# Two results of an MLP block scaled in two units, and the recurrent part's first preparations put one block earlier

## The chip, the cores and the metric

The kernel runs on one core of a Trainium2 chip. The core has TensorE (matrix products, PE in the profile; its weight loads are PEld), VectorE (DVE), ScalarE (ACT), GpSimd (POOL) and SyncE (SP), each with its own queue of instructions, and 16 DMA engines. The metric is the time of one execution in microseconds (us), as the median of several runs.

## The reference

Two mixers over the same 2048 rows of 512 numbers, joined by a gate. Cut to what matters:

```
g = sigmoid((x * gate_w).sum(-1))
a = A(x)          # recurrent attention: 64 segments of 32 rows, 32 heads of 128
b = B(x)          # layernorm, 512 -> 1376, gelu, 1376 -> 512
return g * a + (1 - g) * b

A: mem = mem0                                  # 8 memory rows
   for each segment xs:
       h = concat(mem, xs)                     # 40 rows
       q, k, v = h @ Wq, h @ Wk, h @ Wv
       o = softmax(mask(q @ k.T * scale)) @ v @ Wo
       mem, out = o[:8], o[8:]
```

The segments depend on one another through the memory rows, so A is a chain of 64 steps. B and the gate have no such chain.

## The kernel before, in words

The order of all instructions is written out by hand: an engine takes them in the order in which the program issues them, and waits only where data or a buffer isn't ready. There are two parts. First comes the MLP (B) together with the gates, some 98 us long, during which the weights of A are loaded; then the loop of 64 steps, about 10.4 us each.

**The MLP.** It goes in 8 blocks (`blk`, 0 to 7) of two tiles of 128 rows. A block has 11 units (`fc`, 0 to 10), one for each 128 of the 1376 hidden numbers. A unit does two things (loop over `units`):
- `a_mm(blk, fc)`: four products into PSUM bank SbF or W, by turns (line 460), then ScalarE's GELU from that bank into hTm (line 461). The bank is free again when the GELU has read it, so the products of unit n + 2 wait for the GELU of unit n.
- `b_mm` of the unit two before (LAG = 2): two products (line 466), one for each tile, added up over the 11 units in two of the four banks U. Even blocks use U[0] and U[1], odd ones U[2] and U[3].

A block's last `b_mm` thus stands in unit 1 of the next block. There the two results are scaled by 1 - g and written to SBUF as `ct` (ScalarE, line 473), and stored to the scratch tensor `c_dr` by a DMA that GpSimd issues (line 476). In the last block VectorE scales (line 475) and SyncE issues the store.

Other work is put between the units. In unit 0: ScalarE's tanh for the gates of the block before (line 449) with two small VectorE steps, then `prep` for the next block: statistics of its two tiles, a reciprocal square root in small steps, and the normalized tiles y (line 432), all on VectorE. In units 6 and 7: `prep_tr` (7 and 8 in block 0), the transposes of y on TensorE into banks X1 and X2 (line 439), which VectorE copies to yT (line 440). In unit 8: `loads`, which issues transfers of later tiles and of A's weights on SyncE's queue. In block 3 these include the first two transposed tiles xT (line 94) and the memory rows m0 (line 346).

**What leads over to the loop.** Of each segment's 32 rows, 24 ride with the 8 memory rows in one 32-column tile hT; the last 8 ("left rows") of four segments are gathered into a tile GL and multiplied together. The generator `first()` does the preparations for the first four segments in the last block, as side work between the units:
- its first piece, in unit 1: four small transposes of m0 into X1 (line 481); VectorE's copy of them into hT (line 482) is put into a list that is emptied right after; `left_x` for two tiles (the copies of left rows into GL by GpSimd, line 99); `prep_h(0)`, the copy of 24 rows into the first hT by GpSimd (line 237);
- then 24 pieces of four products each (`left_v`, line 139, and `left_qk`, line 120), six groups of four pieces, in banks X1, X2, U[0], X1, X2, U[0]. The table `(0, 1, 1, 0, 0, 8, 0, 8, 0, 8, 0)` says how many pieces each unit takes: one in unit 1, one in unit 2, eight in units 5, 7 and 9.

**The loop.** Each step projects hT to q, k and v, does the scores, the exponentials, the weighted sums and the product with Wo, and writes the new memory into the next hT. The left rows of later tiles are side work in it.

The code of the functions that the change touches, with the line numbers that the profile uses:

Of the kernel before, what the change touches and what calls it, by code (L numbers as in the profile page):

```python
# [10 lines left out]
BF16 = mybir.dt.bfloat16  # L11
I32 = mybir.dt.int32
ACTF = mybir.ActivationFunctionType
ALU = mybir.AluOpType
# [13 lines left out]
def kernel(ctx, tc, A_x, A_mem0, A_Wq, A_Wk, A_Wv, A_Wo, A_seg_len, B_x, B_w1, B_b1, B_w2, B_b2, gate_w, out):  # L28
    nc = tc.nc
    P = 128  # L30
    _, S, Dm = A_x.shape
# [15 lines left out]
    RIDE = 32 - M  # L47
# [3 lines left out]
    scale = float(Dh) ** -0.5  # L51
# [12 lines left out]
    c_dr = dram.tile([S, Dm], BF16, name="c_dr")  # L64
# [6 lines left out]
    hT = [ep.tile([P, KC, 32], BF16, name=f"hT{i}") for i in range(3)]  # L71
# [19 lines left out]

    def load_xT(T):
        xT = ew.tile([P, KC, P], BF16, tag="xT", bufs=3, name="xT")
        nc.sync.dma_start_transpose(out=xT[:], in_=x2[T * P:(T + 1) * P, :])
        xTs[T] = xT

    def left_x(T):
        GL = ew.tile([P, KC, LEFT, SPT], BF16, tag="GL", name="GL")
        nc.gpsimd.tensor_copy(out=GL[:].rearrange("p k c i -> p k i c"), in_=xTs[T][:].rearrange("p k (i t) -> p k i t", i=SPT)[:, :, :, RIDE:seg])
        GLs[T] = GL  # L100

# [55 lines left out]
    dve_q, act_q = [], []  # L157

    def flush(q, n=1):
        for _ in range(min(n, len(q))):  # L160
            q.pop(0)()
# [4 lines left out]
    def left_qk(T, t, hf, bk):  # L166
        for kc in range(KC):
            qk_unit(bk, gl(T), t, hf, kc)
            if kc < KC - 1:
                yield  # L170
        def ca():
            Tb = qk_cast(bk[:])
            dve_q.append(lambda: qk_tr(Tb, QL[T % 2], hf) if t == 0 else kl_tr(Tb, T, hf))
        act_q.append(ca)
        yield
# [6 lines left out]
    def left_v(T, vb, bk):  # L182
        if vb == 0:
            VLs[T] = ew.tile([P, 4, 2, Dh], BF16, tag="VL", bufs=1, name="VL")
        for kc in range(KC):
            v_unit(bk, gl(T), vb, kc)
            if kc < KC - 1:
                yield

        def ca():  # L190
            VL = VLs[T]
            nc.scalar.copy(out=VL[:, :, vb, :], in_=bk[:].rearrange("p (a e) -> p a e", a=4))

            if vb == 1:
                vp_load(T, 0)
        act_q.append(ca)
        yield
# [37 lines left out]
    def prep_h(s):  # L235
        T, si = divmod(s, SPT)
        nc.gpsimd.tensor_copy(out=hT[s % 3][:, :, 0:RIDE], in_=xTs[T][:, :, seg * si:seg * si + RIDE])
# [54 lines left out]
    with tc.tile_pool(name="mlpw", bufs=1) as mlpw, \  # L292
         tc.tile_pool(name="mwork", bufs=2) as mwork, \
         tc.tile_pool(name="msmall", bufs=2) as msmall:
        TB = 2
        NBLK = NT // TB
# [9 lines left out]
        def ld_x(T, eng=nc.sync):  # L306
            xt = mwork.tile([P, Dm], BF16, tag="xt", bufs=6, name="xt")
            eng.dma_start(xt[:], x2[T * P:(T + 1) * P, :])
            xts[T] = xt

        def ld_w(W_, A, n):
            nc.sync.dma_start(W_[:, n, :], A[n * P:(n + 1) * P].rearrange("p h e -> p (h e)"))

        def ld_o(i):
            nc.sync.dma_start(Wo_sb[:, i:i + 8, :], A_Wo[i:i + 8].rearrange("h e d -> e h d"))
# [23 lines left out]
        def loads(blk):  # L339
            if 2 * blk + 7 < NT:  # L340
                ld_x(2 * blk + 6)
                ld_x(2 * blk + 7)
            if blk == 3:
                for T in range(2):
                    load_xT(T)
                nc.sync.dma_start(m0[:], A_mem0[0])

            for kc in range(2 * blk, min(2 * blk + 2, 3 * KC)):
                ld_w(*((Wv_sb, A_Wv), (Wq_sb, A_Wq), (Wk_sb, A_Wk))[kc // KC], kc % KC)
            if blk == 6:  # L350
                for i in range(0, H, 8):
                    ld_o(i)
# [46 lines left out]
        omg = mlpw.tile([P, NT], FP32)  # L399
# [42 lines left out]
        def gate_sums(blk):  # L442
            for T in range(blk * TB, blk * TB + TB):
                junk = mwork.tile([P, Dm], BF16, tag="junk", bufs=1, name="junk")
                nc.vector.scalar_tensor_tensor(out=junk[:], in0=xts.pop(T)[:], scalar=1.0, in1=gw_bc[:], op0=ALU.mult, op1=ALU.mult, accum_out=z_all[:, T:T + 1])

        def gates(blk):
            t0, t1 = blk * TB, blk * TB + TB
            nc.scalar.activation(out=th[:, t0:t1], in_=z_all[:, t0:t1], func=ACTF.Tanh, scale=0.5)
            nc.vector.tensor_scalar(out=g_all[:, t0:t1], in0=th[:, t0:t1], scalar1=0.5, scalar2=0.5, op0=ALU.mult, op1=ALU.add)  # L450
            nc.vector.tensor_scalar(out=omg[:, t0:t1], in0=th[:, t0:t1], scalar1=-0.5, scalar2=0.5, op0=ALU.mult, op1=ALU.add)

        def bp(blk, tt):
            return U[2 * (blk % 2) + tt]

        def a_mm(blk, fc):
            rows = min(P, F - fc * P)
            hp = (SbF, W)[(blk * FC + fc) % 2]
            for kc in range(KC):
                nc.tensor.matmul(hp[:rows, 0:TB * P], lhsT=w1_sb[:, kc, fc * P:fc * P + rows], rhs=yTs[blk][:, kc, :], start=(kc == 0), stop=(kc == KC - 1))  # L460
            nc.scalar.activation(out=hTm[blk % 2][:rows, fc, :], in_=hp[:rows, 0:TB * P], func=ACTF.Gelu_apprx_tanh, bias=b1_sb[:rows, fc:fc + 1], scale=1.0)

        def b_mm(blk, fc):
            rows = min(P, F - fc * P + 1)
            for tt in range(TB):
                nc.tensor.matmul(bp(blk, tt)[:], lhsT=hTm[blk % 2][:rows, fc, tt * P:(tt + 1) * P],  # L466
                                 rhs=w2_sb[:rows, fc, :], start=(fc == 0), stop=(fc == FC - 1))
            if fc == FC - 1:
                for tt in range(TB):
                    T = blk * TB + tt  # L470
                    ct = mwork.tile([P, Dm], BF16, tag="ct", bufs=4, name="ct")
                    if blk < NBLK - 1:
                        nc.scalar.activation(out=ct[:], in_=bp(blk, tt)[:], func=ACTF.Copy, scale=omg[:, T:T + 1])
                    else:
                        nc.vector.tensor_scalar(out=ct[:], in0=bp(blk, tt)[:], scalar1=omg[:, T:T + 1], scalar2=None, op0=ALU.mult)
                    (nc.gpsimd if blk < NBLK - 1 else nc.sync).dma_start(c_dr[T * P:(T + 1) * P, :], ct[:])

        def first():
            m0p = X1[:].bitcast(BF16)[:, 0:KC * M].rearrange("p (k m) -> p k m", k=KC)
            for kc in range(KC):  # L480
                nc.tensor.transpose(m0p[:, kc, :], m0[:, kc * P:(kc + 1) * P], ident[:M, :M])
            dve_q.append(lambda: nc.vector.tensor_copy(out=hT[0][:, :, RIDE:32], in_=m0p))
            for T in range(2):
                left_x(T)
            prep_h(0)
            yield
            bks = (X1, X2, U[0], X1, X2, U[0])
            for n, (v, t, hf) in enumerate(((1, 0, 0), (1, 0, 1), (0, 0, 0), (0, 1, 0), (0, 0, 1), (0, 1, 1))):
                yield from (left_v(0, hf, bks[n]) if v else left_qk(0, t, hf, bks[n]))
# [15 lines left out]
        for n, (blk, fc) in enumerate(units):  # L505
            a_mm(blk, fc)
            if n == len(units) - 1:
                dummy = msmall.tile([P, 1], FP32, tag="dummy", name="dummy")
                nc.scalar.activation(out=dummy[:], in_=omg[:, 0:1], func=ACTF.Exp)
            if n >= LAG:  # L510
                b_mm(*units[n - LAG])
            if fc == 0:
                if blk >= 1:
                    gates(blk - 1)
                if blk + 1 < NBLK:
                    prep(blk + 1)
                else:
                    gate_sums(blk)
            if blk + 1 < NBLK:
                f0 = 7 if blk == 0 else 6  # L520
                if fc in (f0, f0 + 1):
                    prep_tr(blk + 1, fc - f0)
                if fc == f0 + 1:
                    gate_sums(blk)
                if fc == 8:
                    loads(blk)
                if fc == 9:
                    next(cgen, None)
            elif fc >= 1:
                if fc == 1:  # L530
                    side0 = first()
                if fc == 3:
                    gates(blk)
                for _ in range((0, 1, 1, 0, 0, 8, 0, 8, 0, 8, 0)[fc]):
                    next(side0, None)
                    flush(act_q, 9)
                    flush(dve_q, 9)
# [108 lines left out]
    for s in range(nseg):  # L646
        T, si = divmod(s, SPT)
# [254 lines left out]
```

## Time and profile before

| | |
|---|---|
| median of 3 runs | 780.51 us (779.76 to 783.5) |
| the profiled execution | 779.49 us |
| its span, first to last instruction | 777.7 us |
| TensorE busy | 761.1 us (98%) |
| ScalarE busy | 529.5 us (68%) |
| VectorE busy | 345.1 us (44%) |
| GpSimd busy | 278.7 us (36%) |
| mean granted TensorE clock | 0.997 of full speed |

Times in the views count from the first instruction. A row of the timeline has the start, the length, the engine, the line, the instruction with its output and inputs, and in brackets the idle time of the engine before it and what ended that. "x2" in such a row merges two instructions into one stretch. Matmuls are pipelined, so the length of a merged row is longer than the time until the next row starts. In the view of groups, a row ends with the busy time in all and the mean of one in ns. In the view of stretches, a row has the length, then the busy time of each engine (PE, PEld, DVE, ACT, POOL), the clock, the DMA share and GB/s. In the table of waits the three numbers are the time in all, the times and the longest.

### The profile page before, as it was taken

The numbers are of one execution on the slowest core, as the hardware profiler recorded it, in microseconds if no ns is written. First come the engines' busy times: TensorE is split into PE (matmuls) and PEld (weight loads), VectorE is DVE, ScalarE is ACT, GpSimd is POOL, SyncE is SP. The second block draws the span as 40 slices with busy tenths as digits, with TensorE's granted clock in tenths as the row PEclk, the third lists the DMA queues.
The fourth block names the chain that finished last, engine by engine and source line by source line (L and its number), as shares of the span: only waits on it lengthen the run. The fifth ranks groups of instructions, "written<-read, shape, count | busy, mean of one in ns | idle before, by whom it ended". The sixth has DMA issues, their size and how long they took to land.

```text
span 777.7 us, 44316 instructions
## 1 busy us (share of the span) xinstructions
PE 761.1 (98%) x19687; PEld 420.3 (54%) x19687; DVE 345.1 (44%) x1235; ACT 529.5 (68%) x1439; POOL 278.7 (36%) x523
## 2 busy tenths in 40 slices
PE   7999999999999999999999999999999999999996
PEld 5666555555555555555555555555555555555553
DVE  5776254344435343434443443534343444444334
ACT  4666576777777677777777677767777777777663
POOL 4111033433443433344433334434324443343342
PEclk9999999999999999999999999999999999999999
DMA  6779412212122222212221212222231212121221
GB/s 195 271 245 390 139 58 62 75 61 79 62 62 71 79 72 68 80 52 72 62 88 61 89 62 56 67 79 72 71 80 58 70 54 88 62 82 62 66 62 48
DMA packets 53174, 70.61 MB, mean 91 GB/s; under 512 B 21289, under 2 KB 42898, under 8 KB 51442
## 3 DMA queue, kind: packets, MB, share of 16 engines
q1 hardware_dynamic: 51250, 64.84, 26.0%
q8 instruction: 156, 2.56, 1.3%
q0 software_dynamic: 784, 1.97, 0.7%
q10 hardware_dynamic: 944, 0.92, 0.3%
q14 instruction: 40, 0.33, 0.1%
HBM read 56.96 MB, written 4.45 MB: 79 GB/s over the span
## 4 chain that ended last, share of the span: by engine, by line
PE 87%; DVE 1%; ACT 0%; issue 0%; DVEq 0%
PE U L120 29%; PE X L139 18%; PE W L151 15%; PE X L120 8%; PE X L151 4%; PE U L281 3%; PE U L640 2%; PE U L268 1%; PE W L257 1%; PE SbF L257 1%; PE W L249 1%; PE SbF L600 1%; PE SbF L249 1%; PE U L286 1%; PE U L466 1%; PE U L221 0%
## 5 line engine op out<-in xcount | busy, mean ns | idle before, releaser
L626 POOL TENSOR_TENSOR UT<-XR,Rb 128x384 bf16<-128x384 bf16 x126 | 140.1, 1133 | 296.2 <-DMA Rb<-r_dr 215.9
L125 ACT CAST Tb<-U 128x512 bf16<-128x512 f32 x258 | 150.8, 585 | 76.3 <-PE U L120 75.3
L120 PEld LDWEIGHTS <-hT 128*32 128x32 bf16 x4096 | 104.6, 96 | 109.3 <-DVE hT L642 16.3
L139 PE MATMUL X<-Wv_sb,hT 128*32 128x512 bf16 x2048 | 151.2, 379 | 0.0
L120 PE MATMUL U<-Wq_sb,hT 128*32 128x512 bf16 x2048 | 133.3, 380 | 0.5 <-DVE hT L642 0.2
L120 PE MATMUL U<-Wk_sb,hT 128*32 128x512 bf16 x2048 | 132.7, 379 | 0.0
L151 PE MATMUL W<-Wo_sb,UT 128*32 128x512 bf16 x2080 | 125.2, 380 | 1.3 <-ACT UT L718 1.2
L642 DVE CAST hT<-U 128x16 bf16<-128x16 f32 x126 | 21.9, 175 | 206.0 <-PE U L640 198.3
L129 DVE STREAM_TRANSPOSE QT<-Tb 128x256 f32<-128x256 f32 x128 | 57.0, 446 | 80.8 <-ACT Tb L125 80.7
L151 PEld LDWEIGHTS <-UT 128*32 128x32 bf16 x2080 | 59.4, 96 | 55.6 <-issue 16.3
L606 ACT CAST XR<-U 128x256 bf16<-128x256 f32 x252 | 78.6, 438 | 0.0
L129 DVE STREAM_TRANSPOSE KT<-Tb 128x256 f32<-128x256 f32 x128 | 57.0, 446 | 46.2 <-ACT Tb L125 46.0
L633 ACT CAST w<-W 128x256 bf16<-128x256 f32 (+1 forms) x128 | 41.9, 378 | 47.3 <-PE W L151 47.3
L626 POOL TENSOR_TENSOR UL<-XR,Rb 128x128 bf16<-128x128 bf16 x126 | 60.4, 503 | 0.0
L618 POOL TENSOR_TENSOR racc<-racc,R 128x72 f32<-128x72 f32 x63 | 21.2, 337 | 107.1 <-PE U L286 75.0
L139 PEld LDWEIGHTS <-hT 128*32 128x32 bf16 x2048 | 48.2, 94 | 21.0
L718 ACT CAST UT<-U 128x64 bf16<-128x64 f32 x252 | 35.3, 227 | 28.3 <-PE U L286 28.3
L710 ACT CAST V<-X 128x512 bf16<-128x512 f32 x64 | 37.4, 585 | 22.5 <-PE X L139 22.5
L466 PE MATMUL U<-w_sb,hTm 128*128 128x512 bf16 (+1 forms) x176 | 52.7, 383 | 0.0
L460 PEld LDWEIGHTS <-w_sb 128*128 128x128 bf16 (+1 forms) x352 | 34.2, 101 | 20.5 <-issue 3.2
L696 ACT CAST V<-X 128x512 bf16<-128x512 f32 x64 | 37.5, 585 | 9.5 <-PE X L139 1.1
L125 ACT CAST Tb<-X 128x512 bf16<-128x512 f32 x62 | 36.9, 595 | 7.8 <-PE X L120 6.0
(159 smaller groups left out, 1168.4 us busy)
## 6 DMA issues: line engine op xcount, KB each, us to landing
Rb<-r_dr SPq DMA_DIRECT2D x63, 512.0 KB, 3.9
Wv_sb<-in_A_Wv_dram SPq DMA_DIRECT2D x4, 1024.0 KB, 7.5
Wq_sb<-in_A_Wq_dram SPq DMA_DIRECT2D x4, 1024.0 KB, 7.2
Wk_sb<-in_A_Wk_dram SPq DMA_DIRECT2D x4, 1024.0 KB, 9.2
Wo_sb<-in_A_Wo_dram SPq DMA_DIRECT2D x4, 1024.0 KB, 15.1
VP<-VL SPq DMA_DIRECT2D x64, 64.0 KB, 3.2
c<-c_dr SPq DMA_DIRECT2D x16, 128.0 KB, 3.2
out_dram<-o SPq DMA_DIRECT2D x16, 128.0 KB, 2.7
```

The source lines that it names most:

```text
L120: nc.tensor.matmul(bk[32 * j:32 * j + 32, :], lhsT=G[:, kc, :], rhs=W5[t][:, kc, h0:h1, j, :], start=(kc == 0), stop=(kc == KC - 1), tile_ ...
L125: nc.scalar.copy(out=Tb[:], in_=bk.rearrange("p (a b e) -> p a e b", a=8, b=2))
L129: nc.vector.transpose(out=dst[:, 8 * hf:8 * hf + 8, c0:c0 + 32, :].rearrange("p a r b -> p a (r b)").bitcast(FP32), in_=Tb[:].rearrange("p ...
L139: nc.tensor.matmul(bk[32 * j:32 * j + 32, :], lhsT=G[:, kc, :], rhs=Wv5[:, kc, 4 * vb:4 * vb + 4, j, :], start=(kc == 0), stop=(kc == KC - ...
L151: nc.tensor.matmul(bk[32 * c:32 * c + 32, :], lhsT=U_[:, j, i, :], rhs=Wo_sb[:, 4 * i + j, :], start=(n == 0), stop=(n == NW - 1), tile_po ...
L466: nc.tensor.matmul(bp(blk, tt)[:], lhsT=hTm[blk % 2][:rows, fc, tt * P:(tt + 1) * P], rhs=w2_sb[:rows, fc, :], start=(fc == 0), stop=(fc = ...
L606: nc.scalar.copy(out=XR[:, j], in_=U[j][:, 0:NG * 40].rearrange("p (i q) -> p i q", q=40)[:, :, 0:32])
L626: nc.gpsimd.tensor_tensor(out=out[:, :, 4 * h:4 * h + 4, o:o + b - a], in0=XR[:, :, 4 * h:4 * h + 4, a:b], in1=Rb[:, h, :, :, a:b], op=ALU ...
L633: nc.scalar.copy(out=w[:, a:a + Dm // parts], in_=W[:, a:a + Dm // parts])
L696: nc.scalar.copy(out=v_out(V, 0), in_=X1[:])
L710: nc.scalar.copy(out=v_out(V, 1), in_=X2[:])
L718: nc.scalar.copy(out=UT[s % 2][:, j, :, 0:M], in_=U[j][:, 0:NG * 40].rearrange("p (i q) -> p i q", q=40)[:, :, 32:40])
```

## The change

Two things are put elsewhere; no instruction is added or taken away.

First, of a finished block's two results (blocks 0 to 6) the first is scaled and stored where both were, in unit 1 of the next block. The second goes into the list `late`, which is emptied one unit later, in unit 2, behind that unit's `a_mm` with its GELU and ahead of its `b_mm`. The last block still does both at its end.

Second, what was the first piece of `first()` becomes `first_h()`, and is called in unit 4 of block 6, behind that unit's products, instead of unit 1 of block 7. VectorE's copy into hT is issued there directly. The table for block 7 now has no pieces in units 1 and 2, so the 24 pieces of four products lie eight each in units 5, 7 and 9.

```
             if fc == FC - 1:
-                for tt in range(TB):
-                    T = blk * TB + tt
-                    ct = mwork.tile([P, Dm], BF16, tag="ct", bufs=4, name="ct")
-                    if blk < NBLK - 1:
-                        nc.scalar.activation(out=ct[:], in_=bp(blk, tt)[:], func=ACTF.Copy, scale=omg[:, T:T + 1])
-                    else:
-                        nc.vector.tensor_scalar(out=ct[:], in0=bp(blk, tt)[:], scalar1=omg[:, T:T + 1], scalar2=None, op0=ALU.mult)
-                    (nc.gpsimd if blk < NBLK - 1 else nc.sync).dma_start(c_dr[T * P:(T + 1) * P, :], ct[:])
-
-        def first():
+                if blk < NBLK - 1:
+                    ct_out(blk, 0)
+                    late.append(lambda: ct_out(blk, 1))
+                else:
+                    for tt in range(TB):
+                        ct_out(blk, tt)
+
+        late = []
+
+        def ct_out(blk, tt):
+            T = blk * TB + tt
+            ct = mwork.tile([P, Dm], BF16, tag="ct", bufs=4, name="ct")
+            if blk < NBLK - 1:
+                nc.scalar.activation(out=ct[:], in_=bp(blk, tt)[:], func=ACTF.Copy, scale=omg[:, T:T + 1])
+            else:
+                nc.vector.tensor_scalar(out=ct[:], in0=bp(blk, tt)[:], scalar1=omg[:, T:T + 1], scalar2=None, op0=ALU.mult)
+            (nc.gpsimd if blk < NBLK - 1 else nc.sync).dma_start(c_dr[T * P:(T + 1) * P, :], ct[:])
+
+        def first_h():
             m0p = X1[:].bitcast(BF16)[:, 0:KC * M].rearrange("p (k m) -> p k m", k=KC)
             for kc in range(KC):
                 nc.tensor.transpose(m0p[:, kc, :], m0[:, kc * P:(kc + 1) * P], ident[:M, :M])
-            dve_q.append(lambda: nc.vector.tensor_copy(out=hT[0][:, :, RIDE:32], in_=m0p))
+            nc.vector.tensor_copy(out=hT[0][:, :, RIDE:32], in_=m0p)
             for T in range(2):
                 left_x(T)
             prep_h(0)
-            yield
+
+        def first():
             bks = (X1, X2, U[0], X1, X2, U[0])
...
             a_mm(blk, fc)
...
+            while late:
+                late.pop(0)()
             if n >= LAG:
                 b_mm(*units[n - LAG])
...
                     loads(blk)
+                if blk == NBLK - 2 and fc == 4:
+                    first_h()
...
-                for _ in range((0, 1, 1, 0, 0, 8, 0, 8, 0, 8, 0)[fc]):
+                for _ in range((0, 0, 0, 0, 0, 8, 0, 8, 0, 8, 0)[fc]):
                     next(side0, None)
```

## The prediction

> **What bounds the kernel now.** I write (b,f) for unit f of MLP block b. First the page: TensorE works almost without a break, 98% of a span of 777.7 us, at a granted clock that no slice shows below 9 tenths. So time is gained only where TensorE stands still.
>
> ```profile
> span 777.7 us, 44316 instructions
> PE 761.1 (98%) x19687; PEld 420.3 (54%) x19687; DVE 345.1 (44%) x1235; ACT 529.5 (68%) x1439; POOL 278.7 (36%) x523
> PEclk9999999999999999999999999999999999999999
> ```
>
> Second, TensorE's waits in the first 160 us (time in all, times, longest). One row lies near the change: 1.5 us, once, for GL, the first left rows that GpSimd copies at line 99. No wait for an eviction of the scaled results (ct, line 473) is listed.
>
> ```profile
> PE X L139 <- POOL GL L99: 1.5, 1, 1.5
> ```
>
> Third, the timeline of that place, (7,1) and (7,2): start, length, engine, line, instruction.
>
> ```profile
> 80.79 0.60 PE L466 MATMUL U<-w_sb,hTm 97*128 97x512 bf16 x2
> 81.32 0.25 PE L481 MATMUL X<-ident,m 8*128 8x8 bf16 x4
> 81.50 0.61 PE L460 MATMUL W<-yT,w_sb 128*128 128x256 bf16 x4
> 81.95 0.59 PE L466 MATMUL U<-w_sb,hTm 128*128 128x512 bf16 x2
> 82.40 1.12 POOL L476 DMA_DIRECT2D c_dr<-ct  x2 [9.02 <-ACT ct L473]
> 83.56 0.74 POOL L99 COPY GL<-xT 128x128 bf16<-128x128 bf16 x2
> 84.08 0.40 PE L139 MATMUL X<-Wv_sb,GL 128*32 128x512 bf16 x4 [1.53 <-POOL GL L99]
> 84.11 0.27 POOL L237 COPY hT<-xT 128x96 bf16<-128x96 bf16 x1
> 84.41 0.61 PE L460 MATMUL SbF<-yT,w_sb 128*128 128x256 bf16 x4
> ```
>
> GpSimd issues two stores of ct (1.12 us), which wait for ScalarE's two evictions, and only then copies GL. TensorE meets its first left product at (7,2) and stands until the first copy is done. Its inputs are not late: the loads of xT started at 48.9 and 50.2 us and took at most 4.1, that of the memory rows started at 51.5.
>
> ```profile
> L94 SPq DMA_TRANSPOSE xT<-in_A_x_dram x2: 1242/1282/1322, 48.9 to 50.2; - x2
> DMA to landing us min/median/max: 2.8/3.5/4.1
> L346 SPq DMA_DIRECT2D m<-in_A_mem_dram x1: 480/480/480, 51.5 to 51.5; - x1
> ```
>
> Fourth, an ordinary block, here block 6. Blocks repeat to 0.02 us, so one stands for blocks 2 to 6.
>
> ```profile
> 28.80:38.95 10.15, 10.15 (x75) 6.96 (x74) 7.29 (x31) 6.19 (x15) 1.08 (x2) 1.00 0.74 259
> 69.36:79.49 10.13, 10.13 (x76) 6.95 (x74) 6.70 (x26) 6.23 (x15) 1.08 (x2) 1.00 1.05 376
> ```
>
> ```profile
> 70.65 0.17 DVE L450 TENSOR_SCALAR g_all<-th 128x2 f32<-128x2 f32 x1 [1.93 <-ACT th L449]
> ...
> 71.29 1.26 ACT L473 ACTIVATE ct<-U,omg 128x512 bf16<-128x512 f32 x2
> 71.96 0.60 PE L460 MATMUL W<-yT,w_sb 128*128 128x256 bf16 x4
> 72.27 1.12 POOL L476 DMA_DIRECT2D c_dr<-ct  x2 [9.02 <-ACT ct L473]
> 72.40 0.59 PE L466 MATMUL U<-w_sb,hTm 128*128 128x512 bf16 x2
> 72.43 0.48 ACT L461 ACTIVATE hTm<-SbF,b_sb 128x256 bf16<-128x256 f32 x1
> 72.79 0.49 ACT L461 ACTIVATE hTm<-W,b_sb 128x256 bf16<-128x256 f32 x1
> 72.97 0.60 PE L460 MATMUL SbF<-yT,w_sb 128*128 128x256 bf16 x4
> 73.40 0.59 PE L466 MATMUL U<-w_sb,hTm 128*128 128x512 bf16 x2
> 73.83 0.60 PE L460 MATMUL W<-yT,w_sb 128*128 128x256 bf16 x4
> 74.98 0.74 DVE L432 TENSOR_SCALAR y<-xt,mv,rs 128x512 bf16<-128x512 bf16 x2
> 75.14 0.59 PE L466 MATMUL U<-w_sb,hTm 128*128 128x512 bf16 x2
> 75.45 0.33 PEld L439 LDWEIGHTS <-y 128*128 128x128 bf16 x4 [0.21 <-DVE y L432]
> 75.57 0.39 PE L439 MATMUL X<-ident,y 128*128 128x128 bf16 x4
> ```
>
> A unit is two halves of 0.43 us, 0.87 in all (72.97 to 73.40 to 73.83). From 71.96 to 72.97 are 1.01 us: the products of (6,4) want bank SbF, whose GELU stood behind both ct and ended at 72.91 (72.43 + 0.48). That stall is 0.14 us. But look on: the transposes of y for the next block start at 75.57, right behind (6,6) (75.14 + 0.43), and their weight load had waited for y until 75.45. VectorE reaches y by a chain of small steps that begins right after ScalarE's tanh at the block's start (70.65) and runs for 4.3 us until the first y; a TensorE that is earlier at (6,6) waits for y.
>
> **The change part by part.** Nothing is added but order.
>
> *One ct moved behind the GELU of the next unit, blocks 1 to 5.* ScalarE's pitch is 0.57 for ct (71.29 to 72.43 for two), 0.36 for a GELU (72.43 to 72.79). The GELU of (b,2) then starts at 71.86 instead of 72.43, the second ct at 72.22, the GELU of (b,3) at 72.79 as now: it ends at 73.28, and its bank is wanted at 73.70. So the 0.14 stall goes. What is late next is y: the load can't start before 75.45, and its 0.1 us, which today lies under the matmuls, shows; the first useful effect is at about 75.55 against 75.57. Value 0.02 a block, five blocks: -0.1. Bounds: 0 and -0.7 (five times the whole 0.14). The store of the second ct comes some 0.4 us later on GpSimd's queue, where nothing but the moved copies stands behind it.
>
> *Memory transposed in block 6.* At (7,1) the four transposes cost 81.50 - 80.79 - 0.43 = 0.28 us; that goes: -0.28. At (6,4) the same 0.28 comes. There the products start at 72.83, the transposes follow at 73.80, and TensorE is ready for y's transposes at 75.72. These write X1, which VectorE must first have emptied of the memory rows. That copy (line 482, 170 ns) is queued behind both y: it starts about 0.33 us (the pitch of the two in 0.74, one taking 411) behind the second one's start, at 75.64, ends at 75.81, and the release reaches TensorE some 0.06 later (as from the first y's end, 74.98 + 0.41, to the load at 75.45), 75.87. So the transposes start at 75.87 instead of 75.57: +0.30. Bounds: +0.14 (0.28 less the stall, no wait for X1) and +0.77 (a y delayed by one GL copy, below).
>
> ```profile
> L432 DVE TENSOR_SCALAR y<-xt,mv,rs 128x512 bf16<-128x512 bf16 x4 | 1.5, 411 | 0.1
> L99 POOL COPY GL<-xT 128x128 bf16<-128x128 bf16 x2 | 0.7, 470 | 0.0
> L482 DVE COPY hT<-X 128x32 bf16<-128x32 bf16 x1 | 0.2, 170 | 0.0
> ```
>
> *GL and first hT copied in block 6.* GpSimd is idle there but for the stores of ct: today they start 0.3 us behind the first ct's end (72.27, against 71.29 + 1.26 - 0.57); counted the same way from the second ct's new end (72.22 + 0.69), the second store runs from 73.2 to 73.75. The three copies, 0.82 us now (83.56 to 84.38), then run to about 74.6. First use is at (7,5), over ten units later: nothing on the path. The cover that hides them is that distance; without it they would cost what (7,2) shows. SP's queue is not touched.
>
> *First left step taken out of (7,2).* From the end of the second half (81.95 + 0.43 = 82.38) to the next products at 84.41 are 2.03 us: the wait of 1.53, the work, and the changes of array shape on both sides. The work doesn't vanish; the sides take 8 steps each at units 5, 7 and 9, and unit 9 gets one step more than its seven. 28 products from 87.12 to 88.64 make 54 ns each, a step of four 0.22. Net -1.81; bounds -1.53 (the wait alone) and -1.81.
>
> ```profile
> 87.12 1.70 PE L139 MATMUL X<-Wv_sb,GL 128*32 128x512 bf16 x28
> 88.64 0.39 PE L120 MATMUL U<-Wq_sb,GL 128*32 128x512 bf16 x4
> ```
>
> What the standstill covered lies bare at (7,4): the late GELU would now stall it by 0.14, and the moved ct prevents just that, so nothing is added.
>
> Sum: -0.1 + 0.30 - 0.28 - 1.81 = -1.9 us, bounds -1.0 and -2.6. The profiled execution took 779.49 us and would take 777.6. The median of the runs, 780.51, is 1.0 above it, and the prediction is for the median: 778.6.
>
> **The rivals.** *The split pays in full:* y is not what TensorE waits for, because its chain moves too. Against it is the 0.21 us wait for y at 75.45. Then 0.14 - 0.02 more in five blocks, 0.6: 778.0.
>
> *A GL copy in y's way:* if GpSimd starts its copies late, a 470 ns copy could lie on y's start at 74.98, and y's transposes come 0.47 later: 779.1. By the sum GpSimd is done 0.4 us earlier; no row shows both at once. The Trainium skill (SBUF — State Buffer, Who interferes with whom) says that GpSimd shares a port pair with VectorE in its two-port modes, and that whoever issues second is blocked for the whole instruction; the trace of before cannot show this, since here the two never met.
>
> *The standstill moves on:* something that the wait at (7,2) hid stops TensorE for the same 1.53 later in block 7: sum -0.4, 780.1. Against it: apart from GL, none of TensorE's waits between 76 and 98 us is listed.
>
> *Slower:* the loop of 64 steps is entered 1.9 us earlier, with its transfers in another phase. In some steps the last matmul runs straight into the next step; in others hT comes last, for 0.19 us. These rows of the chain (start, us, what) show one of each:
>
> ```profile
> 108.42 0.45 PE X L120 x8
> 108.87 3.45 PE U L120 x64
> ...
> 129.13 0.19 DVE hT L642
> ```
>
> Ten more such steps eat the gain, 31 more make it slower by 0.5%; with half the steps, 32, it is 6.1 - 1.9 = 4.2 us slower: 784.7. Against it: the step's end hangs on its own Wo products, not on how the loop was entered. *Its mirror:* eleven steps fewer with that wait, -2.1 more: 776.5.
>
> **How the numbers follow.** Forecast 0.54; split in full 0.15; GL on y 0.08; standstill moves 0.11; slower 0.07, of which 0.05 over 0.5%; mirror 0.05. Half a per cent is 3.9 us, about what a measurement of this kernel can tell from no change; all but the last two lie within it: faster 0.05, same 0.90, slower 0.05. The range takes in the forecast with its bounds, the split and the moved standstill, and half a microsecond of scatter: 776.8 to 780.6.
>
> **What would show it.** Right: no wait of TensorE for GL; (b,4) 0.87 behind (b,3) in every block, yet blocks 2 to 5 no shorter than 10.1 us; y's transposes of block 6 about 0.3 later in their block, held by X1; (7,2) an ordinary unit; the loop's first step 1.9 us earlier, its length from there the same. Wrong: blocks of 10.0 us (the split paid), y starting late in block 6, a new wait in block 7, or a loop whose length differs by more than a microsecond.

## The result, and the profile after

The kernel after takes 778.81 us (median of 20 runs, 777.18 to 780.24) where the kernel before, beside it, takes 780.76 (20 runs). The ratio is 0.997, with a 95% interval of 0.9962 to 0.9979: faster by 0.3%, 1.95 us between the medians. The profiled execution took 779.11 us, with a span of 777.3. That is only 0.4 us less than the profiled execution before, because this one execution spent 1.6 us more in the loop; the section on the prediction comes back to it. The MLP's part of the trace is steadier, and carries the comparison.

Of TensorE's waits in the first 160 us, GL is gone from the list, and a short one has come, for the copy of the memory rows (now line 491) out of X1:

```profile
PE X L439 <- DVE hT L491: 0.2, 1, 0.2
```

The view of stretches. A row goes from one block's first product to the next one's, and the last row of each view from block 7's first product to the loop's first mask product. Before: block 5 and the stretch from block 7 on (block 6, 10.13, stands in the prediction). After: blocks 2, 5 and 6, and the stretch from block 7 on.

```profile
59.22:69.36 10.14, 10.14 (x76) 6.96 (x75) 6.70 (x26) 6.24 (x15) 1.08 (x2) 1.00 1.02 397
79.49:97.97 18.48, 16.95 (x171) 8.84 (x169) 4.14 (x16) 10.91 (x23) 1.90 (x5) 1.00 0.35 112
```

```profile
28.69:38.72 10.03, 9.98 (x74) 6.88 (x74) 7.29 (x30) 6.17 (x15) 1.08 (x2) 1.00 0.72 261
58.77:68.80 10.03, 9.93 (x74) 6.89 (x74) 6.70 (x26) 6.23 (x15) 1.08 (x2) 1.00 1.01 390
68.80:79.48 10.68, 10.39 (x78) 7.03 (x78) 7.05 (x27) 6.23 (x15) 1.91 (x5) 1.00 1.05 376
79.48:95.86 16.38, 16.22 (x165) 8.85 (x166) 4.13 (x15) 10.80 (x23) 1.08 (x2) 1.00 0.39 123
```

So an ordinary block is shorter by 0.10 to 0.11 us, block 6 longer by 0.55 (10.68 against 10.13), and the last stretch shorter by 2.10. Block 6 after, in the timeline: the products of (6,4) at 72.28 come 0.87 behind those of (6,3), without the stall; the transposes of the memory rows cost the 0.28 forecast; then y's transposes stand until 75.56.

```profile
71.41 0.60 PE L460 MATMUL W<-yT,w_sb 128*128 128x256 bf16 x4
72.28 0.60 PE L460 MATMUL SbF<-yT,w_sb 128*128 128x256 bf16 x4
73.05 0.16 DVE L410 SCALAR_TENSOR_TENSOR rs<-nt,rs 128x2 f32<-128x2 f32 x1
73.23 0.76 POOL L99 COPY GL<-xT 128x128 bf16<-128x128 bf16 x2
73.24 0.25 PE L490 MATMUL X<-ident,m 8*128 8x8 bf16 x4
73.25 0.29 DVE L408 TENSOR_TENSOR nt<-rs 128x2 f32<-128x2 f32 x1
73.57 0.24 DVE L409 SCALAR_TENSOR_TENSOR nt<-nt,ve 128x2 f32<-128x2 f32 x1
73.84 0.23 DVE L410 SCALAR_TENSOR_TENSOR rs<-nt,rs 128x2 f32<-128x2 f32 x1
74.69 0.74 DVE L432 TENSOR_SCALAR y<-xt,mv,rs 128x512 bf16<-128x512 bf16 x2
75.16 0.10 PEld L439 LDWEIGHTS <-y 128*128 128x128 bf16 x1 [0.32 <-DVE y L432]
75.34 0.17 DVE L491 COPY hT<-X 128x32 bf16<-128x32 bf16 x1
75.56 0.38 PE L439 MATMUL X<-ident,y 128*128 128x128 bf16 x4 [0.23 <-DVE hT L491]
```

Three small VectorE operations that take 0.16 us elsewhere take 0.23 to 0.29 while GpSimd copies GL beside them, and y starts 74.69 - 68.80 = 5.89 us into its block. In block 5 of the same trace it is 64.40 - 58.77 = 5.63:

```profile
64.40 0.73 DVE L432 TENSOR_SCALAR y<-xt,mv,rs 128x512 bf16<-128x512 bf16 x2
64.86 0.23 PEld L439 LDWEIGHTS <-y 128*128 128x128 bf16 x4 [0.34 <-DVE y L432]
64.87 0.40 PE L439 MATMUL X<-ident,y 128*128 128x128 bf16 x4
```

### The profile page after: what moved, and what is told of

Same layout as the page of the kernel before. It is cut to its first block, busy times and chain, and to the rows that moved or that the text cites. A ratio compares the mean times of both kernels' runs of the same rounds, so it can differ in the third digit from the quotient of the medians.

```text
span 777.3 us, 44300 instructions
## 1 busy us (share of the span) xinstructions
PE 759.5 (98%) x19673; PEld 419.6 (54%) x19687; DVE 345.4 (44%) x1235; ACT 529.6 (68%) x1439; POOL 278.6 (36%) x523
## 4 chain that ended last, share of the span: by engine, by line
PE 96%; DVE 2%; issue 1%; DMA 1%; ACT 0%; POOL 0%; DVEq 0%; ACTq 0%; POOLq 0%
PE U L120 29%; PE X L139 18%; PE W L151 15%; PE X L120 7%; PE U L466 4%; PE X L151 4%; PE U L281 3%; PE SbF L460 2%; PE W L460 2%; PE U L654 2%; PE U L268 1%; PE W L257 1%; PE SbF L257 1%; PE W L249 1%; PE SbF L614 1%
## 5 line engine op out<-in xcount | busy, mean ns | idle before, releaser
L466 PE MATMUL U<-w_sb,hTm 128*128 128x512 bf16 (+1 forms) x163 | 49.5, 381 | 0.6
```

## The experiments

All lengths of stretches are from the view of stretches, which repeats to 0.02 us from execution to execution. A kernel for which no ratio is given was timed once, and such a single time says nothing here: times of one kernel scatter by more than the effects.

**The whole change again.** No edit.

> The whole change once more, beside the kernel with the other bank and two visits: blocks 2 to 5 10.03 us, block 6 10.68, block 7 16.38; 0.3% less than the kernel before, and 0.6 us more than its neighbour, which timing alone will hardly tell apart. The MLP's stretches should repeat to 0.02 us, the loop's length by a microsecond or two.

Measured: ratio 0.9981 (0.9967 to 0.9994); blocks 2 to 5 10.02 to 10.04, block 6 10.69, block 7 16.38. The stretches repeat, and the gain is there a second time.

**Each part alone.** First the split without the move:

```
-            nc.vector.tensor_copy(out=hT[0][:, :, RIDE:32], in_=m0p)
+            dve_q.append(lambda: nc.vector.tensor_copy(out=hT[0][:, :, RIDE:32], in_=m0p))
...
         def first():
+            first_h()
+            yield
...
-                if blk == NBLK - 2 and fc == 4:
-                    first_h()
...
-                for _ in range((0, 0, 0, 0, 0, 8, 0, 8, 0, 8, 0)[fc]):
+                for _ in range((0, 1, 1, 0, 0, 8, 0, 8, 0, 8, 0)[fc]):
```

> Only the second ct is moved one unit on; memory, left rows and first hT stay in block 7. Theory (in block units 1 to 4 the late GELU is all that stands in TensorE's way, and y lets nearly all of it through): blocks 2 to 6 take 10.03 us instead of 10.14, no more waits at (b,4). In block 7 GpSimd now has only one store of ct ahead of the GL copies, since the second is issued a unit later: TensorE's wait for GL falls from 1.5 to about 0.9. The loop's first mask product, at 97.97 us before, comes at about 96.8; time 0.15% less. Rival, as predicted (y takes the gain back): blocks 10.11, loop at about 97.3.

Measured: ratio 0.9991 (0.9978 to 1.0004), not told apart from no change by time alone. Stretches of blocks 5 and 6, and from block 7 on, and the new wait:

```profile
59.15:69.18 10.03, 9.93 (x74) 6.87 (x75) 6.71 (x26) 6.25 (x15) 1.08 (x2) 1.00 1.02 417
69.18:79.21 10.03, 9.98 (x75) 6.88 (x75) 6.70 (x26) 6.24 (x15) 1.08 (x2) 1.00 1.05 376
79.21:97.12 17.91, 16.80 (x169) 8.85 (x171) 4.15 (x16) 11.04 (x23) 1.84 (x5) 1.00 0.38 121
```

```profile
82.12 0.54 POOL L485 DMA_DIRECT2D c_dr<-ct  x1 [8.54 <-ACT ct L482]
82.70 0.74 POOL L99 COPY GL<-xT 128x128 bf16<-128x128 bf16 x2
83.22 0.40 PE L139 MATMUL X<-Wv_sb,GL 128*32 128x512 bf16 x4 [0.95 <-POOL GL L99]
```

The theory held: the split alone brings blocks to 10.03, and since only one store stands ahead of GL, the wait falls to 0.95. That y would take nearly all of the gain back is refuted.

Then the move without the split:

```
-                    late.append(lambda: ct_out(blk, 1))
+                    ct_out(blk, 1)
```

> Only memory, left rows and first hT are put into block 6; both ct stay together. Theory: blocks 2 to 5 stay at 10.14 us; block 6 takes 10.68 as with the whole change, because its length is set by the release of X1, which hangs on VectorE and not on TensorE's place; block 7 to the loop's first mask product takes 16.38 and 0.14 for the late GELU at (7,4), 16.5. The loop starts at about 96.5 (before 97.97, with the whole change 95.86); time 0.19% less. Rival (the two parts are independent, block 6 longer by the transposes alone): block 6 10.42, loop at 96.3.

Measured: ratio 0.9986 (0.9972 to 1.0000), at the edge of no change by time alone.

```profile
59.23:69.37 10.14, 10.03 (x74) 6.95 (x75) 6.70 (x26) 6.24 (x15) 1.08 (x2) 1.00 1.01 389
69.37:79.90 10.53, 10.48 (x79) 7.03 (x79) 6.90 (x27) 6.23 (x15) 1.92 (x5) 1.00 1.06 374
79.90:96.41 16.51, 16.35 (x166) 8.84 (x167) 4.06 (x15) 10.80 (x23) 1.08 (x2) 1.00 0.36 117
```

Blocks and the last stretch came as expected, with the 0.14 of the late GELU bare at (7,4). Block 6 did not: 10.53, neither 10.68 nor 10.42. With both stores together the copies of GL start at another point of VectorE's chain, 4.07 us into the block instead of 4.43, and two operations are slowed instead of three, so that y starts 5.74 us into the block:

```profile
73.43 0.16 DVE L409 SCALAR_TENSOR_TENSOR nt<-nt,ve 128x2 f32<-128x2 f32 x1
73.44 0.76 POOL L99 COPY GL<-xT 128x128 bf16<-128x128 bf16 x2
73.62 0.16 DVE L410 SCALAR_TENSOR_TENSOR rs<-nt,rs 128x2 f32<-128x2 f32 x1
73.82 0.21 DVE L408 TENSOR_TENSOR nt<-rs 128x2 f32<-128x2 f32 x1
74.06 0.22 DVE L409 SCALAR_TENSOR_TENSOR nt<-nt,ve 128x2 f32<-128x2 f32 x1
```

The operations at 73.43 and 73.62 lie beside the first copy of GL and keep their 0.16 us. So not every operation that meets a copy is slowed, and what decides it stays open.

From the first product of block 1 to the loop's first mask product, the split saves 1.2 us and the move 1.6, both together 2.05. The parts overlap by 0.7: most of it, 0.57, because each of them shortens the wait for GL, and 0.12 because beside the move the split costs 0.15 in block 6 (10.68 against 10.53) where alone it saves 0.10, less the 0.13 that it gives back at (7,4).

**What stops block 6.** The four transposes into another bank:

```
-            m0p = X1[:].bitcast(BF16)[:, 0:KC * M]...
+            m0p = U[3][:].bitcast(BF16)[:, 0:KC * M]...
```

> The whole change, with the four memory transposes of unit 4 in block 6 going to bank U[3], which is free there, instead of X1; VectorE's and GpSimd's work stays where it is. Theory: y's transposes no longer wait for VectorE's copy of the memory rows; y itself is still some 0.26 us late, since GpSimd's copies slow VectorE's small steps, but TensorE is late by as much: block 6 takes 10.30 us instead of 10.68. Rival (y's own lateness is what counts, not X1): block 6 stays above 10.5.

```profile
69.13:79.43 10.30, 10.25 (x78) 6.96 (x78) 7.06 (x27) 6.23 (x15) 1.91 (x5) 1.00 1.06 373
```

Measured 10.30: the wait for X1 was worth 0.38 us, and without it only the transposes' 0.27 over an ordinary block are left.

The whole step at unit 9 instead of unit 4:

```
-                if blk == NBLK - 2 and fc == 4:
+                if blk == NBLK - 2 and fc == 9:
```

> The whole change, with the memory, left rows and first hT put in unit 9 of block 6 instead of unit 4. Theory (of block 6's extra 0.65 us, 0.28 are the four transposes and 0.38 a wait for X1, behind VectorE's y and GpSimd's copies): at unit 9 VectorE has nothing queued and X1 isn't wanted, so block 6 takes 10.03 + 0.28 = 10.31 us instead of 10.68, and the loop starts at 95.5 instead of 95.86. Rival (the transposes themselves cost that much): block 6 stays at 10.68.

Measured: ratio 0.9957 (0.9940 to 0.9974), but block 6 takes 10.61, not 10.31. The timeline shows why: GpSimd's copies did not move.

```profile
74.02 0.75 POOL L99 COPY GL<-xT 128x128 bf16<-128x128 bf16 x2
74.03 0.29 DVE L408 TENSOR_TENSOR nt<-rs 128x2 f32<-128x2 f32 x1
75.48 0.74 DVE L432 TENSOR_SCALAR y<-xt,mv,rs 128x512 bf16<-128x512 bf16 x2
75.95 0.40 PE L439 MATMUL X<-ident,y 128*128 128x128 bf16 x4
79.11 0.25 PE L490 MATMUL X<-ident,m 8*128 8x8 bf16 x4
```

The block begins at 69.58; y starts 5.90 into it, as late as with unit 4, and the transposes of unit 9 come on top. Nothing in GpSimd's queue stands between the last store of ct and the copies, and their inputs are long there, so they run 4.43 to 4.44 us into the block whether the program issues them in unit 4 or in unit 9. The ratio looks better than the whole change's, but its interval overlaps with that, and block 6 moved by 0.07 us only.

Only the copies moved to unit 9:

```
             nc.vector.tensor_copy(out=hT[0][:, :, RIDE:32], in_=m0p)
+
+        def first_x():
             for T in range(2):
                 left_x(T)
             prep_h(0)
...
+                if blk == NBLK - 2 and fc == 9:
+                    first_x()
```

> The whole change, but GpSimd's three copies (left rows, first hT) go to unit 9 of block 6; the four transposes and VectorE's copy stay in unit 4. Theory (GpSimd's copies lengthen the two-input steps of VectorE's chain to y): the steps at lines 408 to 410 all take about 160 ns again, y starts 5.63 us after the block's first product instead of 5.89, and the wait for X1 falls from 0.38 to about 0.15: block 6 takes 10.45 us instead of 10.68. Rival (the long steps come from something else): y still starts at 5.89, block 6 10.68.

Measured: nothing changed (block 6 10.69, y 5.90 into it), for the same reason. This run says nothing on what lengthens VectorE's steps; the next one does. The three copies by VectorE itself, in unit 9:

```
+        def first_x():
             for T in range(2):
-                left_x(T)
-            prep_h(0)
+                GL = ew.tile([P, KC, LEFT, SPT], BF16, tag="GL", name="GL")
+                nc.vector.tensor_copy(out=GL..., in_=xTs[T]...)
...
+            nc.vector.tensor_copy(out=hT[0][:, :, 0:RIDE], in_=xTs[0][:, :, 0:RIDE])
...
+                if blk == NBLK - 2 and fc == 9:
+                    first_x()
```

> The whole change, but the three copies (left rows, first hT) are done by VectorE in unit 9 of block 6, where it is idle, and GpSimd does none of them; the four memory transposes stay in unit 4 with bank X1. (Put into unit 9 for GpSimd, the copies ran at the old place: its queue has nothing in between that waits.) Theory (GpSimd's copies lengthen the two-input steps of VectorE's chain): lines 408 to 410 all take about 160 ns, y starts 5.63 us after the block's first product instead of 5.89, and of the wait for X1 only some 0.15 us are left: block 6 takes 10.45 us instead of 10.68. Rival (the long steps come from TensorE's transposes or from PSUM, not from GpSimd): y at 5.89, block 6 10.68.

```profile
69.11:79.53 10.42, 10.37 (x78) 7.03 (x78) 7.17 (x30) 6.24 (x15) 1.08 (x2) 1.00 1.06 374
```

```profile
73.56 0.25 PE L490 MATMUL X<-ident,m 8*128 8x8 bf16 x4
73.56 0.16 DVE L408 TENSOR_TENSOR nt<-rs 128x2 f32<-128x2 f32 x1
74.74 0.74 DVE L432 TENSOR_SCALAR y<-xt,mv,rs 128x512 bf16<-128x512 bf16 x2
75.61 0.38 PE L439 MATMUL X<-ident,y 128*128 128x128 bf16 x4
```

With TensorE's transposes still there and GpSimd silent, the steps take 0.16 us and y starts 5.63 into the block. So GpSimd's copies are what slowed them, and of block 6's extra 0.65 us over an ordinary block 0.26 go away with that. What is left is 10.42 against 10.13 in the kernel before, +0.29.

**What the wait at (7,2) hid.** The kernel before, with the copies alone issued ahead of block 7:

```
-            for T in range(2):
-                left_x(T)
-            prep_h(0)
             yield
...
+                if blk == NBLK - 2 and fc == 9:
+                    for T in range(2):
+                        left_x(T)
+                    prep_h(0)
```

> The kernel before, with GpSimd's three copies alone put into unit 9 of block 6; the two ct stay together, the memory is transposed in unit 1 of block 7, and the first left piece stays in unit 2. Theory: TensorE's wait for GL, 1.5 us, is gone and nothing takes its place at (7,2), but the late GELU then stalls (7,4) by up to 0.14; blocks as before; block 7 to the loop's first mask product takes 18.48 - 1.55 = 16.9 us. Rival (something else stops TensorE there as soon as GL doesn't): more than 17.5 us.

```profile
81.00:97.90 16.90, 16.74 (x168) 8.86 (x169) 4.13 (x16) 10.92 (x23) 1.08 (x2) 1.00 0.43 138
```

Measured 16.90: the wait alone was worth 1.58 us, and nothing took its place; no wait of TensorE is listed in that stretch.

One piece put back into unit 2:

```
-                for _ in range((0, 0, 0, 0, 0, 8, 0, 8, 0, 8, 0)[fc]):
+                for _ in range((0, 0, 1, 0, 0, 8, 0, 8, 0, 8, 0)[fc]):
```

> The whole change, but with one piece of left products back in unit 2 of block 7, where GL is now there in time. Theory (a visit to products of 32 columns costs a change of shape on both sides, 0.1 us each, beside the work): block 7 to the loop's first mask product takes 16.38 + 0.2 = 16.6 us. Rival (no such cost): 16.38.

Measured 16.60 against 16.38: one more visit to the 32-column products costs 0.22 us beside its work. That this is the change of shape, and how it divides between the two sides, isn't shown by this run.

**Whether y holds TensorE.** One refinement step of the reciprocal square root less:

```
-            for _ in range(3):
+            for _ in range(2):
```

> The whole change, with two steps instead of three in the refinement of the reciprocal square root (blocks 1 to 7), so a less exact reciprocal; VectorE's chain to y is three small operations, some 0.6 us, shorter. Theory (with the late GELU gone, y still holds TensorE for some 0.03 us a block): blocks 2 to 5 take 10.00 us instead of 10.03; block 6, whose X1 is released 0.6 earlier, 10.28 to 10.30 instead of 10.68. Rival (y no longer matters): blocks stay at 10.03.

```profile
59.62:69.62 10.00, 9.89 (x73) 6.96 (x74) 6.21 (x23) 6.23 (x15) 1.08 (x2) 1.00 1.02 403
69.62:79.91 10.29, 10.24 (x78) 7.03 (x78) 6.56 (x24) 6.23 (x15) 1.90 (x5) 1.00 1.05 376
```

Measured 10.00 and 10.29: y does hold TensorE once the late GELU is gone, but for 0.03 us a block.

**A shorter version in the trace.** The other bank, and the left pieces in two visits:

```
+            m0p = U[3][:].bitcast(BF16)[:, 0:KC * M]...
...
-                for _ in range((0, 0, 0, 0, 0, 8, 0, 8, 0, 8, 0)[fc]):
+                for _ in range((0, 0, 0, 0, 0, 12, 0, 0, 12, 0, 0)[fc]):
```

> The whole change, with the memory transposed into bank U[3], and the 24 left pieces taken in two visits of twelve (units 5 and 8) instead of three of eight. Theory: block 6 takes 10.30 us instead of 10.68, as measured for the bank alone; a visit costs 0.2 us in changes of shape beside its work, so block 7 to the loop's first mask product takes 16.18 instead of 16.38. Together 0.6 us less than the whole change, 0.35% less than the kernel before. Rival (longer visits make ScalarE's casts late for the GELUs and stall TensorE): block 7 16.4 or more.

Measured: ratio to the kernel before 0.9960 (0.9943 to 0.9977); block 6 10.30, last stretch 16.14, so a visit less saves 0.24. In the trace it is 0.6 us ahead of the whole change, as expected; the intervals of the two ratios overlap, so timing alone doesn't show that.

## Why the prediction was right

*The sum.* Forecast -1.9 us and 778.6; measured -1.95 between the medians and 778.81, and in the profiled traces -2.05 us from block 1 to the loop. The forecast of a change within half a per cent held. But two terms were off, one to each side: the split brought 0.40 more than its term, block 6 cost 0.25 more. That the sum came out within 0.2 us is luck as far as these two go. Of the signs that the prediction had named against itself, three came: blocks of 10.0 us, y late in block 6, and a loop whose length differs by more than a microsecond. The first two are the two terms; the third is weighed below.

*Block 7 was right.* Forecast -0.28 and -1.81, together -2.09; measured -2.10 (18.48 to 16.38). The parts were measured one by one: 1.58 for the wait, 0.22 for the visit, and 0.27 for the transposes, as block 6 shows them with the other bank. The standstill did not move on.

*The split in blocks 1 to 5 was too small.* Forecast -0.1, measured -0.50 (0.07 in block 1, four times 0.10 to 0.11). The mechanism was right as far as it went: y is what TensorE meets next, 0.03 us a block. The step that failed is the weight load whose 0.1 us would show. Its rows, quoted above for block 5 after, have the load at 64.86 and the first transpose at 64.87: here the transposes did not wait for the load's end. The Trainium skill (TensorE: Matmul & The Clock Gate, Architectural detail: the array is 16× 32×32, not 1× 128×128) says that a matmul can begin before its weight load is complete; this trace agrees, with 0.01 us between the two starts where the load takes 0.10. So the rival in which the split pays in full was nearer than the forecast.

*Block 6 was too cheap.* Forecast +0.30, measured +0.55. The transposes (0.28) and the wait for X1 were foreseen; but the wait was 0.38 where the forecast's rows give 0.15 (75.72 to 75.87), because y came 0.26 late. With the copies made by VectorE, y was not late and block 6 cost +0.29, next to the forecast's +0.30: the path through X1 was right, and only the neighbour was missing. The step that failed is that GpSimd's copies cost nothing on the path: they ended before y started, as forecast, but slowed the small steps that lead to y. The rival had the right kind of cause, in another place and at half its price (0.26 instead of 0.47). The Trainium skill (SBUF — State Buffer, Who interferes with whom) says that a VectorE instruction with two SBUF inputs contends with a GpSimd instruction that reads SBUF, and calls the port pair that the two engines share an exclusive lock. Which operations were hit agrees with that: lines 408 to 410 have two inputs. How much does not agree with a lock held for a whole copy: they grew by 0.05 to 0.13 us beside copies of 0.47, and two that lay beside a copy in the move without the split did not grow at all. That the shared ports are the cause is thus not shown; that GpSimd's copies are, is.

*The loop.* It was longer in the profiled execution, but within its scatter, so the rival in which the loop slows has no support here. From its first mask product to the last step's it took 658.5 us in the trace before and 660.1 after, but the same loop took 656.6 to 660.2 in the eleven other traces. Steps of one kind differ by up to 0.8 us within the trace after, and by up to 1.1 in one of the others. Part of this is single stops of TensorE marked "issue", that is, with no releaser in the trace. These are the stops within the loop's steps in the table of waits, first of after, then of before:

```profile
PE X L151 <- issue: 0.7, 2, 0.5
PE W L151 <- issue: 0.6, 2, 0.5
PE X L139 <- issue: 0.5, 1, 0.5
PE W L261 <- issue: 0.2, 1, 0.2
```

```profile
PE X L120 <- issue: 0.3, 1, 0.3
```

After lost 2.0 us to them, before 0.3, and the difference is about what its loop took longer. The other traces go the same way: the four of all thirteen in which such stops lost more than 1 us within the loop took 659.2 to 660.2 us there, the seven with less than 0.4 took 656.6 to 658.5, and the whole change run again took 659.3, so the length doesn't go by the kernel alone. What makes these stops stays open. They are a reason why one profiled execution says little about the time of a change of this size.

## What to carry to other kernels

Read a wait by what stands ahead in the releasing engine's queue: here two stores in front of three small copies cost TensorE 1.6 us, and taking the copies out from behind them brought three quarters of the gain (1.56 of 2.05 us). When a step is moved, look not only at the engine that waits but at what else its engines and its bank do at the new place: a scratch bank that is wanted soon, and a neighbour engine's copies beside a chain of small steps, cost 0.4 us together, and another bank gave that back. And an instruction that is issued later in the program runs later only if its own queue has something in between: GpSimd's had nothing between units 4 and 9, and its copies stayed where they were.

## What had not been expected of the hardware

GpSimd's copies in SBUF lengthened VectorE's two-input operations of 128x2 numbers from 0.16 us to between 0.21 and 0.29, though not every one that met a copy; they did not hold them for the copy's 0.47. A weight load that TensorE must wait for delayed the first transpose by 0.01 us, not by its own 0.10. A visit from products of 128 columns to products of 32 and back costs 0.22 to 0.24 us beside its work.
